# All element-wise sums on one engine, an unused set of sums left out, and a new order drawn by the kernel's own planner

## The chip, the core and the metric
The kernel runs on one core of a Trainium2 chip. The core has five engines with instruction streams of their own: TensorE (PE in the profile, with PEld for its weight loads), VectorE (DVE), ScalarE (ACT), GpSimd (POOL) and SyncE (SP). They meet through semaphores. SBUF is the working memory of 128 partitions, PSUM takes the results of TensorE in eight banks, and transfers from and to the chip's main memory run on 16 DMA engines. The metric is the device time of one execution in microseconds (us).

## The reference
Attention over 8 batches, 12 heads, 448 tokens and a head dimension of 64 is followed by two dense layers with a silu gate between them.
```python
scores = scale * np.matmul(q, k.transpose(0, 1, 3, 2))
attn = exp(scores - max) / (sum + 1e-09)
x = np.matmul(attn, v)            # -> (8 * 448, 768)
h = x @ w_in                      # w_in 768 x 2048
g = h * (1.0 / (1.0 + np.exp(-h)))
out = g @ w_out                   # w_out 2048 x 768
```
Inputs and output are float32; the kernel computes its products in float16 with float32 sums.

## The kernel before
**Tiling.** Attention works on *units*: one batch and four of the heads, 27 units in all, since batch 0 is cut into two pieces of tokens. For a unit, K and Q are loaded (rk, rq), turned on VectorE into KT and QT (L363, L374), multiplied on TensorE into scores (s, L384), and put through exp on ScalarE into tiles E (L409). Each unit has four chunks of keys and so four E tiles. TensorE then multiplies E with a matrix of ones for the row sums and with V for the result (p, L433); VectorE turns the row sums, inverts them, turns them back (t, inv; L455 to L460), and scales the result into xT (L466). Where there is room, the E tiles of chunks 0 and 1 are added first, so that the row sums need one chunk less: that is `plan_esum`, one sum for each half of the heads, 896 columns each.

**First layer.** `Plain` multiplies xT with w_in (p, L486) tile by tile; ScalarE takes tanh (th, L499) and VectorE the gate (G and X, L502).

**Second layer.** `Quad` makes a block of two times 128 tokens by 768 outputs with seven products for eight (a Strassen scheme). It needs sums of G tiles (S, or E tiles used for S, in `plan_sums`, four kinds of two sums of 512 columns each) and sums of w_out (TO and, in place, w_out_t, in `plan_w_out_sums`, 16 sums of 768 columns). Its results are added on VectorE (t<-p,t and p<-p,t, L511) or copied out of PSUM by ScalarE or VectorE (L515, L517), and stored by SyncE (L546). A similar scheme for the first layer, `Fold`, exists in the code with its sums of w_in (SI and, in place, w_in_t, in `plan_w_in_sums`, 32 sums of 384 columns), but it is for batches from `PLAIN` = 8 on, and there are eight batches, 0 to 7: no Fold runs.

**Order.** The program's instructions are put out in an order that a planner in the kernel draws at build time. `Order` keeps a clock for each engine; every `Op` has a cost, dependencies and a bias. TensorE is given work by the main loop: score products when they are ready and the pace allows, then attention results, then the first open item of the two layers. Each engine then runs its instructions strictly in the order put out, except for waits on semaphores. Kinds of operations in the planner: "DVE", "ACT", "POOL", "ANY" (ScalarE or VectorE) and "VP" (VectorE or GpSimd, whichever is free first in the planner). In the kernel before, E sums (`ESENG`), sums of weights (`WENG`) and the third and fourth kind of S sums (`VPS`) are "VP". All sums go through one helper, `tt`, so all have line L511; they are told apart by their tiles.

**Loads.** All loads are issued by GpSimd, in one list (`plan_k`, `plan_q`, `plan_v`, `plan_w_in`, `plan_w_out`), when nothing else is ready for GpSimd in the planner. The planner takes a load to land 1.5 us and size/0.37 after its issue or after the one before it, and 1.0 later; sizes of K and Q are multiplied by 1.2. w_out is loaded in two halves, in front of unit `W_OUT_AT` (12) and `W_OUT_AT + W_OUT_GAP` (14).

Of the kernel before, what the change touches and what calls it, by code (L numbers as in the profile page):

```python
# [17 lines left out]
HOP = 0.10  # L18
DMA_RATE = 0.37
DMA_TAIL = 1.0  # L20
# [3 lines left out]


# [54 lines left out]
class Op:  # L80


    def __init__(self, eng, busy, emit, deps=(), bias=0.0, tail=HOP, then=None, table=None):
        self.eng, self.busy, self.emit = eng, busy, emit
        self.deps, self.bias, self.tail, self.then = list(deps), bias, tail, then
        self.table = table
        self.done = None
# [5 lines left out]
class Order:  # L93


    def __init__(self):
        self.now = 0.0
        self.free = {"PE": 1.2, "ACT": 2.1, "DVE": 1.2, "POOL": 1.2}
        self.wait = {"ACT": [], "DVE": [], "ANY": [], "POOL": [], "VP": []}
        self.pool = []  # L100
        self.dma_free = 0.0
        self.out = []
        self.mode = None
        self.table, self.loose = 0, True
        self.busy = {e: 0.0 for e in self.free}

    def add(self, op):
        self.wait[op.eng].append(op)
        return op

# [3 lines left out]
    def start(self, op, eng=None):  # L114
        eng = eng or op.eng
        busy = op.busy[eng] if isinstance(op.busy, dict) else op.busy
        if isinstance(op.busy, dict):
            self.emit(lambda: op.emit(eng))
        else:
            self.emit(op.emit)  # L120
        if op.table is not None:
            if op.table != self.table:
                self.table = op.table
                busy += TABLE
        self.free[eng] = self.now + busy
        self.busy[eng] += busy
        op.done = self.now + busy + op.tail
        if op.then:
            op.then(op.done)
# [7 lines left out]
    def load(self, mb, emit, ring=None):  # L137
        op = Op("POOL", 0.58, emit)
        self.pool.append((op, mb, ring))
        return op  # L140

    def step(self):

        soon = []
        for eng in ("ACT", "DVE"):
            if self.free[eng] > self.now:
                soon.append(self.free[eng])
                continue
            best, other = None, None
            for kind in (eng, "ANY") if eng == "ACT" else (eng, "ANY", "VP"):  # L150
                for op in self.wait[kind]:
                    at = op.ready()
                    if at is None:
                        continue
                    if at > self.now:
                        soon.append(at)
                    elif eng == "ACT" and op.table not in (None, self.table):
                        if (other is None or at < other[0]) and (self.table == 0 or self.loose):
                            other = (at, op)
                    elif best is None or at + op.bias < best[0]:  # L160
                        best = (at + op.bias, op)
            if other:
                best = other if not best or self.table == 0 and other[0] < self.now - PATIENCE else best
                if best is not other:
                    soon.append(other[0] + PATIENCE + 0.01)
            if best:
                self.wait[best[1].eng].remove(best[1])
                self.start(best[1], eng)
                soon.append(self.free[eng])
        work = None  # L170
        for kind in ("POOL", "VP"):
# [12 lines left out]
        elif self.pool:  # L184
            op, mb, ring = self.pool[0]
            at = 0.0
            if ring is not None:
                at = ring()
            if at is not None and at <= self.now:
                self.pool.pop(0)  # L190
                self.start(op)
                self.dma_free = max(self.dma_free, self.now + 1.5) + mb / DMA_RATE
                op.done = self.dma_free + DMA_TAIL
                soon.append(self.free["POOL"])
            elif at is not None:
                soon.append(at)
# [4 lines left out]
def kernel(  # L201
# [10 lines left out]

# [20 lines left out]
    DEFER, DITEM = .3, .1  # L233
    SUMS, EKEEP, ESENG = (0, 1), 2, 'VP'
# [9 lines left out]
    W_OUT_AT = NG * len(PIECES) + 6  # L244
    W_OUT_GAP = 2
# [21 lines left out]
    SI = {m: const.tile([128, HC, DFF // 2], FP16, name=f"SI{m}") for m in (1, 2, 4)}  # L267
# [5 lines left out]
    T_s = const.tile([128, 3, HC, S // 2], FP16, name="T")  # L273
    f_s = [const.tile([128, 3, S // 2], FP32, name=f"f_{i}") for i in range(NF)]
# [7 lines left out]
    def bank(i):  # L282
        return P_s[i // 2][:, 0] if i < 4 else B_s[i - 4]
# [16 lines left out]
    def rows_of(n, c):  # L300
        return KROWS[c] if form(*units[n][:2]) == "lone" else 128

# [114 lines left out]
    def attend(n, part, a, es, sums):  # L417
# [6 lines left out]
        for c in chunks:  # L424
            rest = c == NCH - 1 and what != "lone"
# [159 lines left out]
    def plan_k(b, hg):  # L585
        ld_k[(b, hg)] = od.load(1.2 * MB * TPP, lambda: load_k(b, hg), ringed("rk"))

    def plan_q(n):
        ld_q[n] = od.load(1.2 * MB * (units[n][3] - units[n][2]), lambda: load_q(n), ringed("rq"))
# [101 lines left out]
    VPS = (3, 4)  # L691
    WENG = 'VP'
# [14 lines left out]
    def bulk(out, u, w, how, deps, bias):  # L707
# [7 lines left out]
        return od.add(Op(WENG, busy, lambda eng: tt(out, u, w, how, eng), deps, bias))  # L715
# [34 lines left out]
    plan_w_in_sums()  # L750
# [3 lines left out]
    class Quad:  # L754
# [59 lines left out]
        def run(self):  # L814
# [5 lines left out]
            if m == 5:  # L820
# [3 lines left out]
                "PE", (i1 - i0) * mm(n), lambda: self.emit(m, a, m in (1, 5, 6), i0, i1), tail=PE_OUT  # L824
# [13 lines left out]
            def add(name, out, x, y, deps, then=None):  # L838
                ev[name] = od.add(
                    Op("DVE", vec(n), lambda: tt(out, x, y, ALU.add), deps, SLOW, then=then)  # L840
                )

            if m == 1:
                ev["p1"] = od.add(
                    Op("ANY", {"ACT": act(n), "DVE": vec(n)}, lambda e: copy(e, p, W), [op], SLOW)
# [5 lines left out]
            elif m == 6:  # L851
                add("y", W, Q, r, [op, ev["c11"]])
            elif m == 7:
# [9 lines left out]
    class Fold:  # L863
# [66 lines left out]
        def run(self):  # L930
# [14 lines left out]
            op = Op("PE", HC * mm(n), lambda: self.emit(m, a, c0, m in (1, 7)), tail=PE_OUT)  # L945
# [3 lines left out]
            def add(name, eng, out, u, w, how, deps, then=None):  # L949
                busy = vec(n) if eng == "DVE" else 0.12 + 0.00215 * n  # L950
                ev[name] = od.add(
                    Op(eng, busy, lambda: tt(out, u, w, how, eng), deps, SLOW, then=then)
# [3 lines left out]
            if m == 5:  # L956
# [4 lines left out]
                        lambda e: copy(e, F[:, 0:2], src), [op], SLOW,  # L961
                    )
                )
            elif m == 6:
                add("y", "DVE", y, A[:, n : 2 * n], p1, ALU.add, [op])
# [3 lines left out]
            elif m == 3:  # L969
                c12 = add("c12", "DVE", A[:, n : 2 * n], A[:, n : 2 * n], p1, ALU.add, [op])  # L970
                self.finish(A[:, 0 : 2 * n], self.f, [c12], True)
            elif m == 4:
                Bq = bank(self.banks[1])[:, 0:n]
                k = self.banks[1]
                c21 = add("c21", "DVE", p5, Bq, p5, ALU.add, [op, ev["z"]], lambda at: banks.give(k, at))
                self.finish(F[:, 1:3].rearrange("p i n -> p (i n)"), self.f + HF, [c21], False)
            if m in (6, 7) and self.at >= 5 and "c22" not in ev:
                Bq = bank(self.banks[1])[:, 0:n]
                add("c22", "DVE", y, Bq, y, ALU.add, [self.last7, ev["y"]] + [ev["z"]])

        def finish(self, src, ff, deps, psum):
# [9 lines left out]
            if b < SILU:  # L991
# [4 lines left out]
                        -0.3, tail=0.2, table=0,  # L996
# [3 lines left out]
                for lo, hi, dst, at in g_parts(b, 0, S):  # L1000
# [7 lines left out]
                            [last, clear], -4,  # L1008
# [5 lines left out]
            for lo, hi, dst, at in g_parts(b, 0, S):  # L1014
# [6 lines left out]
                        deps + [clear], -2, tail=0.2, table=1,  # L1021
# [14 lines left out]
    def plan_t(b):  # L1036
# [12 lines left out]
        def sums(out, u, w, deps):  # L1049
            return od.add(  # L1050
                Op("DVE", half(HC * n), lambda: tt(out, u, w, ALU.subtract), deps, SLOW + 2)
# [40 lines left out]
    def plan_sums(qd):  # L1092
# [7 lines left out]
        while sums_at[qd] < 4:  # L1100
# [16 lines left out]
            for f0 in (0, 4):  # L1117
# [9 lines left out]
                else:  # L1127
# [7 lines left out]
                        deps, SUM,  # L1135
# [7 lines left out]
    def tile_quad(qd):  # L1143
# [34 lines left out]
        def write(r, c, src, place, deps, then):  # L1178
            if r == 0:
# [5 lines left out]
                        deps, -4,  # L1185
# [21 lines left out]
    class Plain:  # L1207
# [20 lines left out]
        def run(self):  # L1228
# [4 lines left out]
            op = Op("PE", 2 * mm(t1 - t0), lambda: ffn1_plain(b, f, t0, t1, a, c0, c0 + 2), tail=PE_OUT)  # L1233
# [7 lines left out]
            done = od.add(Op("ACT", act(t1 - t0), lambda: tanh(x, th), [op], -0.3, tail=0.2, table=0))  # L1241
# [5 lines left out]
            for lo, hi, dst, at in g_parts(b, t0, t1):  # L1247
# [5 lines left out]
                    [done], -4,  # L1253
# [38 lines left out]
    def qk_at():  # L1292
# [6 lines left out]
        s = [max(banks.free[2 * y], banks.free[2 * y + 1]) for y in ys]  # L1299
# [5 lines left out]
    def run_qk():  # L1305
# [17 lines left out]
        )  # L1323
        done = []
# [8 lines left out]
        for y in ys:  # L1333

            def then(at, y=y):
# [11 lines left out]
                    table=0,  # L1347
                )
# [3 lines left out]
        if c in SUMS and c == SUMS[-1] and per_burst(n) == 1 and ys[-1] == 1:  # L1352
            plan_esum(n)
# [3 lines left out]
    def plan_esum(n):  # L1357
# [3 lines left out]
        at = sum_at[n] = e_slots.take(od.now)  # L1361
        made = sum_op[n] = []
        kr = rows_of(n, SUMS[-1])
        nq = 32 * (units[n][3] - units[n][2])
        for y in range(2):
            hs = slice(2 * y, 2 * y + 2)
            for i, c in enumerate(SUMS[1:]):
                u = e_at[n][SUMS[0]] if i == 0 else at
# [5 lines left out]
                            lambda eng, u=u, w=e_at[n][c], hs=hs: tt(  # L1374
                                E_s[at][0:kr, hs, 0:nq], E_s[u][0:kr, hs, 0:nq],
                                E_s[w][0:kr, hs, 0:nq], ALU.add, eng,
                            ),
                            deps, -2,
# [6 lines left out]
    def lent():  # L1385
        if not qk_seq or silu_phase() or LEND and e_slots.when(1) is None:
            return 0, 2
# [9 lines left out]

    def m_when(n):
        more = lent()
        at = sorted(banks.free[i] for i in (*M, *more))[n - 1]  # L1400
        return None if at == NEVER else at

    def m_take():
        more = lent()
        i = min((*M, *more), key=lambda i: (banks.free[i] > od.now, i < 4, banks.free[i]))
        assert banks.free[i] <= od.now
# [3 lines left out]
    def av_data():  # L1410
# [7 lines left out]
        if part == 0 and n in sum_op:  # L1418
            first = len(SUMS) - 1
# [18 lines left out]
    def run_av():  # L1438
# [5 lines left out]
        sums = SUMS if n in sum_op else ()  # L1444
        count = NCH - (len(sums) - 1 if sums and part == 0 else 0)
        op = Op("PE", count * mm(nq) + 0.013, lambda: attend(n, part, a, es, sums), tail=PE_OUT)
# [18 lines left out]
    def after_av(n, part, op, nq, a):  # L1465
        b, hg, g0, g1 = units[n]
        if part == 0:
# [3 lines left out]
            for step, busy in enumerate((nq / 960.0 + 0.13, 0.2, nq / 960.0 + 0.13)):  # L1471
# [5 lines left out]
                    -10,  # L1477
                )
# [4 lines left out]
        else:  # L1483
# [5 lines left out]
            def then(at):  # L1489
# [10 lines left out]
                then=then,  # L1500
            )
# [35 lines left out]
    def moe_pick(hold):  # L1537
# [3 lines left out]
        for item in moe[:60]:  # L1541
# [10 lines left out]
            at = max([at] + room)  # L1552
            need = 0
# [12 lines left out]
        return None, soon  # L1566

# [70 lines left out]
    for _, _, fn in sorted(od.out, key=lambda x: x[:2]):  # L1638
# [31 lines left out]
```

## Time and profile before
| what | us |
|---|---|
| median of 3 runs | 447.63 (444.66 to 449.26) |
| the profiled execution | 442.18 |
| its span in the profile | 440.4 |
| TensorE busy | 410.0 |
| VectorE busy | 288.6 |
| ScalarE busy | 233.8 |
| GpSimd busy | 209.3, of which sums 109.2 and issues of loads the most of the rest |
| granted TensorE clock, mean | 0.979 of full |

The profile gives for each group of instructions its line, engine and operation, output and input tiles, and shape. "Idle before, releaser" is the time in which the engine stood in front of such an instruction, and whose end let it go. Instructions of one engine overlap a little, so durations can add up to more than the time from one start to the next. An instruction's duration includes what it stood inside the engine for a shared resource, which no wait in the list shows.

### The profile page before, as it was taken

The page shows a single profiled execution, that of the slowest core. Times are in us where ns is not written, and L with a number is a line of the kernel's source. Part 1 is how long each engine was busy: PE and PEld are TensorE (multiplying, and loading weights), DVE is VectorE, ACT ScalarE, POOL GpSimd, SP SyncE. Part 2 cuts the span into 40 slices and gives each one's busy share as a digit, 9 for nine tenths or more (in the row PEclk, how much of TensorE's full clock was granted, in tenths as well). Part 3 has the DMA queues.
Part 4 walks back from the last instruction along what each step waited for, and adds up shares of the span by engine and source line. Part 5 has one row for each costly group of instructions (what it writes and reads, how often), then busy time and mean ns, then how long its engine had stood idle before and what let it go on. Part 6 is the DMA issues. An engine that isn't in the chain of part 4 may idle for free.

```text
span 440.4 us, 9748 instructions
## 1 busy us (share of the span) xinstructions
PE 410.0 (93%) x3853; PEld 208.8 (47%) x3853; DVE 288.6 (66%) x565; ACT 233.8 (53%) x356; POOL 209.3 (48%) x277
## 2 busy tenths in 40 slices
PE   8998878999939999999999999999999999899985
PEld 7665544334315434544554434544453555455453
DVE  3536798777899776577557974587559635834751
ACT  3885757788800768466544755456856124214310
POOL 6575898977686354087204951065306100502510
PEclk9998989899988999999999999999999999999999
DMA  7999408599914456056510853118300130022023
GB/s 111 118 152 204 67 6 106 75 183 151 201 28 69 115 89 117 1 75 106 106 49 12 122 93 84 28 18 128 75 1 2 49 92 5 19 66 61 0 50 95
DMA packets 38750, 34.46 MB, mean 78 GB/s; under 512 B 11952, under 2 KB 37936, under 8 KB 38704
## 3 DMA queue, kind: packets, MB, share of 16 engines
q0 software_dynamic: 27952, 22.82, 37.0%
q1 hardware_dynamic: 9984, 10.24, 8.6%
q10 hardware_dynamic: 768, 0.79, 0.7%
q8 instruction: 30, 0.49, 0.4%
q14 instruction: 16, 0.13, 0.1%
HBM read 45.61 MB, written 11.01 MB: 129 GB/s over the span
## 4 chain that ended last, share of the span: by engine, by line
PE 60%; DVE 5%; DMA 2%; SPq 1%; issue 1%; POOL 1%; ACT 0%; DVEq 0%
PE p L486 24%; PE p L805 24%; PE p L433 7%; PE s L384 4%; DVE S L511 2%; DMA rk<-in_k_dram 1%; DVE E L511 1%; SPq L546 1%; DMA out_dram<-t 1%; DVE t L511 0%; POOL V L330 0%; DVE p L511 0%; DVE QT L374 0%; DVE G L502 0%; ACT th L499 0%
## 5 line engine op out<-in xcount | busy, mean ns | idle before, releaser
L409 ACT ACTIVATE E<-s 128x896 f16<-128x896 f32 (+1 forms) x172 | 148.6, 916 | 68.3 <-PE s L384 67.3
L486 PE MATMUL p<-xT,w_in_t 128*128 128x448 f16 (+1 forms) x864 | 156.9, 335 | 4.2 <-DVE G L502 3.2
L486 PEld LDWEIGHTS <-w_in_t 128*128 128x128 f16 x864 | 82.1, 99 | 76.9 <-issue 19.1
L502 DVE SCALAR_TENSOR_TENSOR G<-th,p 128x448 f16<-128x448 f16 (+2 forms) x144 | 75.7, 534 | 54.6 <-ACT th L499 54.1
L499 ACT ACTIVATE th<-p 128x448 f16<-128x448 f32 (+1 forms) x144 | 70.4, 507 | 63.7 <-PE p L486 60.5
L805 PE MATMUL p<-w_out_t,G 128*128 128x384 f16 x304 | 58.0, 327 | 1.9 <-DVE p L511 1.9
L384 PE MATMUL s<-QT,KT 32*128 32x448 f16 (+4 forms) x864 | 56.7, 343 | 3.0 <-ACT E L409 2.6
L511 POOL TENSOR_TENSOR G<-G 128x512 f16<-128x512 f16 x21 | 25.6, 1227 | 64.9 <-DVE S L511 64.3
L805 PEld LDWEIGHTS <-G 128*128 128x128 f16 x416 | 38.6, 98 | 36.1 <-issue 12.0
L330 POOL DMA_DIRECT2D V<-in_v_dram x88 | 48.9, 562 | 13.7 <-PE p L433 8.4
L515 ACT COPY t<-p 128x384 f32<-128x384 f32 x39 | 18.6, 479 | 69.3 <-PE p L805 67.0
L805 PE MATMUL p<-TO,S 128*128 128x384 f16 x192 | 39.3, 340 | 11.1 <-DVE S L511 7.6
L433 PE MATMUL p<-E,V 128*32 128x448 f16 (+2 forms) x848 | 43.9, 344 | 1.4 <-DVE xT L466 1.4
L805 PEld LDWEIGHTS <-S 128*128 128x128 f16 x280 | 25.8, 100 | 37.7 <-issue 15.5
L511 POOL TENSOR_TENSOR E<-E,E 128x896 f16<-128x896 f16 x18 | 34.6, 1922 | 18.0 <-ACT E L409 17.6
L511 DVE TENSOR_TENSOR t<-p,t 128x384 f32<-128x384 f32 x42 | 23.0, 549 | 29.3 <-PE p L805 26.6
L466 DVE SCALAR_TENSOR_TENSOR xT<-p,t 128x448 f16<-128x448 f32 (+1 forms) x53 | 29.8, 565 | 13.4 <-PE p L433 12.3
L384 PEld LDWEIGHTS <-KT 32*128 32x128 f16 (+2 forms) x864 | 17.6, 98 | 30.7 <-issue 29.0
L433 PEld LDWEIGHTS <-V 128*32 128x32 f16 (+1 forms) x864 | 20.3, 98 | 22.5 <-issue 12.4
L363 DVE STREAM_TRANSPOSE KT<-rk 128x256 f32<-128x256 f32 (+3 forms) x48 | 16.7, 385 | 19.6 <-DMA rk<-in_k_dram 19.6
L511 POOL TENSOR_TENSOR G<-X,G 128x512 f16<-128x512 f16 x4 | 4.9, 1216 | 46.2 <-DVE S L511 46.2
L455 DVE STREAM_TRANSPOSE t<-p 128x448 f32<-128x448 f32 (+1 forms) x27 | 15.9, 589 | 14.2 <-PE p L433 14.0
(62 smaller groups left out, 358.2 us busy)
## 6 DMA issues: line engine op xcount, KB each, us to landing
out_dram<-t SPq DMA_DIRECT2D x208, 48.0 KB, 1.6
rk<-in_k_dram POOLq DMA_DIRECT2D x24, 224.0 KB, 4.7
rq<-in_q_dram POOLq DMA_DIRECT2D x21, 224.0 KB, 5.4
w_out_t<-in_moe_w_out_dram POOLq DMA_DIRECT2D x8, 384.0 KB, 8.9
V<-in_v_dram POOLq DMA_DIRECT2D x43, 64.0 KB, 3.3
V<-in_v_dram POOLq DMA_DIRECT2D x40, 48.0 KB, 2.7
w_in_t<-in_moe_w_in_dram POOLq DMA_DIRECT2D x16, 96.0 KB, 4.7
w_in_t<-in_moe_w_in_dram POOLq DMA_DIRECT2D x8, 192.0 KB, 8.0
```

The lines of the kernel that those rows point to most:

```text
L330: nc.gpsimd.dma_start(out=V[32 * x : 32 * (x + 1), hs, 0:count, :], in_=v[b, hs].rearrange("h (i g) d -> i h g d", g=TPP)[:, :, first : fi ...
L363: nc.vector.transpose(out=kt.rearrange("p c x i -> p x c i")[:, x:y, 0:count], in_=t[:, first : first + count * (y - x)].rearrange("p (x c ...
L384: nc.tensor.matmul(out=P_s[s_pair][p0 : p0 + 32 * (x1 - x0), h % 2, at : at + nq], lhsT=KT[(b, hg)][32 * h : 32 * (h + 1), c, x0:x1, :, e] ...
L409: nc.scalar.activation(out=E_s[e_i][0:kr, 2 * y : 2 * y + 2, 0:nk], in_=P_s[s_pair][0:kr, :, 0:nk], func=AF.Exp, scale=attn_scale,)
L433: nc.tensor.matmul(out=bank(a)[32 * h : 32 * (h + 1), 0:nq], lhsT=w, rhs=E_s[sum_at[n] if part == 0 and c in sums else es[c // per_burst(n)]][
L466: nc.vector.scalar_tensor_tensor(out=x_s[xi][:, cc % HC, 32 * g0 : 32 * g1], in0=bank(a)[:, 0:nq], scalar=0.5, in1=t_s[ti][:, 0:nq], op0=A ...
L486: nc.tensor.matmul(out=bank(a)[:, 0 : t1 - t0], lhsT=w_in_t[:, cc, 128 * f : 128 * (f + 1)], rhs=x_s[x_at[(b, cc // HC)]][:, cc % HC, t0:t ...
L499: nc.scalar.activation(out=th, in_=src, func=AF.Tanh)
L502: (nc.vector if eng == "DVE" else nc.gpsimd).scalar_tensor_tensor(out=out, in0=th, scalar=1.0, in1=x, op0=ALU.add, op1=ALU.mult)
L511: e.tensor_tensor(out=out, in0=a, in1=b, op=op)
L515: nc.scalar.copy(out=out, in_=in_)
L805: nc.tensor.matmul(out=bank(a)[:, 0 : self.n], lhsT=lhs(i), rhs=rhs(i), start=(start and i == 0), stop=(i == last), skip_group_check=True,)
```

## The change
1. `ESENG` and `WENG` go from 'VP' to 'DVE', and `VPS` is empty: all sums are on VectorE.
2. `plan_w_in_sums` is called only if `PLAIN < B`, which is false; SI, T and f tiles aren't made.
3. The planner takes a load to land 2.4 us and size/0.4 after its issue, without the later 1.0 and the factor of 1.2, and has at most 8 loads open (`DMA_OPEN`).
[...]
5. w_out is loaded in front of unit 11 and unit 12.
6. E sums are planned by `sums_of` (chunks 0 and 1 for units from 6 on); `DEFER` goes from 0.3 to 0.15; four banks of the score tiles are lent at the end instead of two.

```diff
-DMA_RATE = 0.37
-DMA_TAIL = 1.0
+DMA_RATE = 0.4
+DMA_LAG = 2.4
+DMA_OPEN = 8
...
+    def locked(self, tiles, eng):
+
+        return max((t for i in tiles for e, t in self.lock[i].items() if e != eng), default=0.0)
...
+                    elif self.locked(op.tiles, eng) > self.now:
+                        soon.append(self.locked(op.tiles, eng))
+                    elif eng == "DVE" and op.port and self.port["POOL"] > self.now:
+                        soon.append(self.port["POOL"])
...
-            if ring is not None:
+            if len(self.sent) >= DMA_OPEN and self.sent[-DMA_OPEN] > self.now:
+                at = self.sent[-DMA_OPEN]
+            elif ring is not None:
                 at = ring()
...
-                self.dma_free = max(self.dma_free, self.now + 1.5) + mb / DMA_RATE
-                op.done = self.dma_free + DMA_TAIL
+                self.dma_free = max(self.dma_free, self.now + DMA_LAG) + mb / DMA_RATE
+                op.done = self.dma_free
+                self.sent.append(op.done)
...
-    DEFER, DITEM = .3, .1
-    SUMS, EKEEP, ESENG = (0, 1), 2, 'VP'
+    DEFER, DITEM = .15, .1
+    EKEEP, ESENG = 2, 'DVE'
+    ES2 = 99
+    ES0, ES1 = 6, 99
...
-    W_OUT_AT = NG * len(PIECES) + 6
-    W_OUT_GAP = 2
+    W_OUT_AT = NG * len(PIECES) + 5
+    W_OUT_GAP = 1
...
+    def sums_of(n):
+        if per_burst(n) == 2 or n < ES0:
+            return ()
+        return (0, 1) if n < ES1 else (0, 1, 2) if n < ES2 else (0, 1, 2, 3)
...
-        ld_k[(b, hg)] = od.load(1.2 * MB * TPP, lambda: load_k(b, hg), ringed("rk"))
+        ld_k[(b, hg)] = od.load(MB * TPP, lambda: load_k(b, hg), ringed("rk"))
...
-    VPS = (3, 4)
-    WENG = 'VP'
+    VPS = ()
+    WENG = 'DVE'
...
-    plan_w_in_sums()
+    if PLAIN < B:
+        plan_w_in_sums()
     plan_w_out_sums()
...
         if not qk_seq or silu_phase() or LEND and e_slots.when(1) is None:
-            return 0, 2
+            return 0, 1, 2, 3
```

## The prediction
> **What bounds the kernel now.** I read the table of busy times first, then the busy time of every engine in stretches of 20 us, then the waits, and at each stretch in which TensorE stands, the timeline of the engine it waits for.
>
> ```profile
> PE 410.0 (93%) x3853; PEld 208.8 (47%) x3853; DVE 288.6 (66%) x565; ACT 233.8 (53%) x356; POOL 209.3 (48%) x277
> ...
> PEclk9998989899988999999999999999999999999999
> ```
> TensorE is the bound: 410 of 440.4 us. No other engine is above two thirds. So a faster kernel can only come from the 30.4 us in which TensorE stands, or from the clock, which the second row shows below full speed in single slices of the first third only.
>
> ```profile
> 0.00:20.00 20.00, 17.67 (x317) 14.53 (x321) 7.38 (x26) 11.91 (x14) 10.70 (x23) 1.00 0.83 113
> ...
> 60.00:80.00 20.00, 15.90 (x176) 7.81 (x175) 16.97 (x36) 12.11 (x20) 18.25 (x25) 0.84 0.55 72
> 80.00:100.00 20.00, 20.00 (x222) 7.60 (x214) 14.48 (x33) 15.96 (x23) 16.51 (x25) 0.99 0.97 140
> ...
> 120.00:140.00 20.00, 13.03 (x88) 6.85 (x77) 19.32 (x25) 2.45 (x5) 15.49 (x14) 0.83 0.28 43
> ...
> 420.00:440.40 20.40, 14.12 (x85) 8.10 (x83) 6.93 (x13) 2.39 (x5) 0.93 (x1) 0.96 0.32 78
> ```
> Columns: stretch, length, then busy us of PE, PEld, DVE, ACT, POOL, then granted clock, DMA share, GB/s. TensorE lacks 4.1 us in 60 to 80 and 7.0 us in 120 to 140, both times with VectorE (17.0, 19.3) and GpSimd (18.3, 15.5) nearly full, and both times the clock falls to 0.83 or 0.84. The first 20 us (2.3 lacking, loads at 0.83 of the DMA engines) and the tail (6.3, the last sums and stores) are a matter of start and end.
>
> ```profile
> 121.78 8.40 DVE L511 TENSOR_TENSOR w_out_t<-w_out_t 128x768 f16<-128x768 f16 x1
> 130.11 0.55 DVE L511 TENSOR_TENSOR TO<-w_out_t,TO 128x768 f16<-128x768 f16 x1
> ```
> ```profile
> 121.53 1.64 POOL L511 TENSOR_TENSOR TO<-w_out_t,TO 128x768 f16<-128x768 f16 x1
> 123.13 1.87 POOL L511 TENSOR_TENSOR E<-E,E 128x896 f16<-128x896 f16 x1
> 124.96 1.62 POOL L511 TENSOR_TENSOR TO<-w_out_t,TO 128x768 f16<-128x768 f16 x1
> 126.55 1.62 POOL L511 TENSOR_TENSOR w_out_t<-w_out_t 128x768 f16<-128x768 f16 x1
> 128.14 1.62 POOL L511 TENSOR_TENSOR TO<-w_out_t,TO 128x768 f16<-128x768 f16 x1
> ```
> ```profile
> 131.04 0.82 PE L805 MATMUL p<-TO,S 128*128 128x384 f16 x2 [6.97 <-DVE S L511]
> ```
> This is the heart of it. Start, duration, instruction. A sum over 768 columns takes VectorE 0.55 us; the one that began at 121.78 took 8.40 us and ended 0.4 us after the last of a row of GpSimd sums (128.14 + 1.62 = 129.76). The two S sums queued behind it, and TensorE stood 6.97 us for the first. A VectorE sum of two SBUF tiles waits for GpSimd's sums to stop.
>
> **The change, part by part.** Counts are from the two programs' orders, durations from the groups with shapes apart.
>
> *Sums leave GpSimd.* 82 sums, 109.2 us (groups E 34.6, G 25.6 + 4.9, S 9.3 + 2.4, w_in and SI 18.6, w_out and TO 10.1, E of FFN2 3.7). 20 of them and 12 on VectorE (8.3 us) make SI and the difference in w_in, which no matmul reads: they go. The other 62 go to VectorE: 20 of E at 0.61 us (the sum at 71.06, before GpSimd began one) = 12.2; 38 of 512 columns at 0.41 = 15.6; 6 of 768 at 0.55 = 3.3. Ten copies out of PSUM also go from ScalarE to VectorE, 10 x 0.545 = 5.5. Together +36.6.
>
> *VectorE's own sums get short.* Mean now less the unhindered duration, times the count: E 18 x (1.213 - 0.61) = 10.9; S<-S,G 20 x (0.835 - 0.41) = 8.5; S<-G 24 x 0.145 = 3.5; w_out 10.5 - 3 x 0.55 = 8.9; the smaller groups 5.8. Sum 37.6. So VectorE's total goes 288.6 + 36.6 - 8.3 - 37.6 = 279, and GpSimd's to about 100: VectorE takes over all sums and is busy for less.
>
> *What of it is TensorE's.* Stalls with a GpSimd sum as their cause, from the timelines of the three engines:
> - 124.1 to 131.0: 6.97, shown above.
> - 59.5 to 62.7: 3.20. The gates (G, L502) stood behind two SI sums of 3.01 us together, held up by POOL's own SI and E sums. These SI sums are unused.
> - 48.3 to 50.0: 1.66, for an E sum on GpSimd (1.87 us; on VectorE 0.61).
> - 380 to 384.5 and 416 to 422: 1.94, 0.58 and 1.59. Behind the last gate of a batch, VectorE does eleven sums before the addition that TensorE waits for; three of each set took 1.37 us against GpSimd's. New order: ten sums at 0.34 from start to start, 3.4 us instead of 5.5. TensorE has 5.2 us of other products there, so I count all 4.1.
> - 251 to 256: 1.06 (an E sum pair of 2.22 us).
> Sum 17.0. To this the clock: after the stall at 131.04, 16 products took 4.69 us where twice 8 take 2.6 (-2.0); after 62.66, 1.3 us more than the same products elsewhere. -3.3. TensorE's own work stays: 3853 to 3832 matmuls, of which 17 are idle filler at the start; switches between the row, column and full forms are 253 and 250 in the two orders.
>
> [...] The row says that VectorE stayed out over five GpSimd sums in a row. [...]
>
> [...] All loads here are issued by GpSimd, and VectorE will do 62 more sums. [...]
>
> *Order with the loads.* GpSimd's stream of loads is the same list, but for w_out, whose first half goes one unit of attention earlier and whose second half two. The cap of 8 and the new rates work only in the planner. It now believes in a k load (0.459 MB in float32) after 2.4 + 0.459/0.4 = 3.5 us, before 4.0; the trace has a median of 4.7 (rq 5.4). So the turns of K and Q stand as early or earlier in VectorE's queue, with gates, S and xT behind them. Now VectorE waits 19.6 us for rk and 2.8 for rq, 16 times. Bounds: it falls to half, since POOL's sums no longer stand in front of the loads (in 50 to 60 the DMA share was 0.01 with POOL 10.0 of 10 busy): -1 on TensorE; or it grows by 27 x 0.5 = 13 us, of which I let TensorE feel a third: +4. I take +1.5. One unit more gets its E sum: 4 matmuls less, -0.2. DEFER, the bank locks and the two more lent banks change which product comes next: -1 to +3, I take +1.5, about the 1% of stalls that the undisturbed stretch from 140 to 376 has (3 us).
>
> Sum: 442.2 (the profiled execution: span 440.4 and 1.8 around it) - 17.0 - 3.3 + 3.0 = 424.9. The three runs shown lie above their profiled one (median 447.6, by 1.2%). Part of that is these blockades, which fall differently in every run; I add nothing but round: **425 us**, 5% under the median.
>
> **Rivals.**
> 1. *The early stage is bound by its loads.* From 84 to 118 the DMA share is above 0.9 in nearly every slice; all of w_out is fetched there beside K, Q and V. If so, TensorE freed at 48 to 63 runs into K and Q that aren't there and gives the 4.9 us and 1.3 us of clock back, and w_out makes the seven at 124 half as large: 425 + 6.2 + 3.5 = 435. For it: w_out now comes with one unit between its halves, 16 us of transfers. Against: in 50 to 60 nothing was being fetched, and TensorE waited 0.3 us in all for a load.
> 2. *Slower.* VectorE, in order, stands at each K and Q turn for a load that the planner believed in 1.2 (k) to 1.9 us too early, and now has every sum behind it. Place: the first turn of each of the 21 whole units. Price: if each costs TensorE 1.6 us, 34 us against 20 gained: 456 in the profiled sum's terms, 460 as a median. It decides from about 1.0 us a unit on, where the gain is eaten. Against: VectorE has 160 us of slack, and with today's 22 us of such waits no wait of TensorE behind a KT or QT row is above 0.4 us.
> 3. *Nothing moves.* TensorE's work is the same, and VectorE's stalls are replaced by ScalarE's: from 40 to 120 ScalarE is busy 60.5 of 80 us, and squeezed into 68 it would be 89%. Then 440 to 446. Against: the new order puts second-layer products, which need no exponentials, into this stage.
>
> **How the numbers follow.** Forecast 0.62 (418 to 432), loads 0.20 (428 to 442), nothing moves 0.09 (440 to 450), slower 0.09 (450 to 465). The range reaches from 415 (the -1 bounds, and the slow clock of 74 to 80 gone too, 3 us, with some 4 us of small waits on VectorE) to 440, the loads' case nearly whole. 1% of the median, 4.5 us, is about what a measurement of this kernel tells from no change: faster (below 443.2) 0.84, within 0.08, slower (above 452.1) 0.08.
>
> **What would show it.** Right: no VectorE sum above 0.7 us; VectorE near 280 and GpSimd near 100 us busy; no stall of TensorE above 2 us between 30 and 425; clock 1.00 in all 20 us stretches after 40. Loads: VectorE's wait for rk above 30 us in the first 130 us. Rival 2: waits of TensorE behind KT or QT rows in every batch. Wrong altogether: a stall as long as those removed with GpSimd idle.

## The result and the profile after

The changed kernel takes 421.08 us (median of 3 runs, 416.86 to 423.8) against 447.63: a ratio of 0.9369, 95% interval 0.9208 to 0.953. A ratio given with an interval is taken from the executions counted as fast alone, so it need not equal the quotient of the medians beside it. Measured again with more runs, the changed kernel takes 421.48 against 445.02, 0.9505 (0.9451 to 0.956). The two intervals share 0.945 to 0.953; I take the gain as about 5%. The profiled execution of the changed kernel (416.86, span 415.1) is the fastest of its three, with a mean granted clock of 0.996, and that of the kernel before (442.18) lies below its three runs.

The table of busy times after, then the rows by stretches of 20 us that answer to those shown before (stretch, length, busy PE, PEld, DVE, ACT, POOL, granted clock, DMA share, GB/s):

```profile
PE 402.2 (97%) x3832; PEld 207.2 (50%) x3832; DVE 274.6 (66%) x627; ACT 229.6 (55%) x346; POOL 101.0 (24%) x195
...
PEclk9899999999999999999999999999999999999999
```
```profile
0.00:20.00 20.00, 16.48 (x246) 13.60 (x246) 6.47 (x24) 8.75 (x10) 9.51 (x21) 0.91 0.79 106
...
60.00:80.00 20.00, 19.96 (x241) 9.40 (x242) 16.25 (x41) 17.20 (x27) 9.68 (x17) 1.00 0.73 103
80.00:100.00 20.00, 19.44 (x184) 8.23 (x176) 17.24 (x41) 13.43 (x20) 9.30 (x17) 1.00 1.15 181
...
120.00:140.00 20.00, 20.00 (x226) 8.27 (x226) 16.42 (x38) 14.37 (x18) 7.59 (x15) 1.00 0.74 117
```
TensorE stands 415.1 - 402.2 = 12.9 us instead of 30.4, of which 3.5 lie in the first 20 us and 4.8 behind 400 us. From 60 to 80 it works 19.96 us of 20 where it worked 15.9. VectorE does all sums and is busy for 14 us less than before.

The sums of one line and engine in the changed kernel: count, then shortest/median/longest in ns, first and last start.

```profile
L541 DVE TENSOR_TENSOR E<-E,E x38: 584/616/626, 39.4 to 319.1; 128x896 f16<-128x896 f16 x38
L541 DVE TENSOR_TENSOR S<-S,G x20: 382/418/426, 70.9 to 395.8; 128x512 f16<-128x512 f16 x20
...
L541 DVE TENSOR_TENSOR w_out_t<-w_out_t x4: 551/556/559, 95.7 to 101.5; 128x768 f16<-128x768 f16 x4
```
The longest equals the median within a few per cent in each group. Before, the w_out sum ranged to 8398 ns. What is left of TensorE's waits from 40 us on, in order of size (us in total, times, longest):

```profile
PE p L516 <- DMA rk<-in_k_dram: 1.1, 1, 1.1
PE p L516 <- DVE G L532: 0.9, 1, 0.9
PE p L516 <- DVE X L532: 0.8, 2, 0.5
PE p L836 <- DVE p L541: 0.8, 1, 0.8
```
None is above 1.1 us, and none has a GpSimd sum behind it.

### The profile page after: what moved, and what is told of

The parts are those of the page before. It is cut to its first block, busy times and chain, and to the rows that moved or that the text cites. A ratio compares the mean times of both kernels' runs of the same rounds, so it can differ in the third digit from the quotient of the medians.

```text
span 415.1 us, 9668 instructions
## 1 busy us (share of the span) xinstructions
PE 402.2 (97%) x3832; PEld 207.2 (50%) x3832; DVE 274.6 (66%) x627; ACT 229.6 (55%) x346; POOL 101.0 (24%) x195
## 4 chain that ended last, share of the span: by engine, by line
PE 84%; DMA 8%; DVE 3%; POOL 2%; issue 1%; ACT 1%; ACTq 0%; DVEq 0%; POOLq 0%
PE p L516 33%; PE p L836 29%; PE p L463 12%; PE s L414 10%; DMA rk<-in_k_dram 4%; DMA V<-in_v_dram 2%; DMA rq<-in_q_dram 2%; POOL V L360 1%; DVE KT L393 1%; DVE G L532 1%; DVE t L541 0%; DVE xT L496 0%; DMA out_dram<-t 0%; PE s L463 0%; ACTq L576 0%
## 5 line engine op out<-in xcount | busy, mean ns | idle before, releaser
L516 PEld LDWEIGHTS <-w_in_t 128*128 128x128 f16 x864 | 81.1, 98 | 74.5 <-issue 14.9
L836 PE MATMUL p<-w_out_t,G 128*128 128x384 f16 x304 | 59.0, 327 | 0.8 <-DVE p L541 0.8
L463 PE MATMUL p<-E,V 128*32 128x448 f16 (+2 forms) x832 | 42.1, 337 | 2.3 <-DMA V<-in_v_dram 1.6
L545 ACT COPY t<-p 128x384 f32<-128x384 f32 x29 | 13.9, 480 | 44.2 <-PE p L836 42.0
L836 PE MATMUL p<-TO,S 128*128 128x384 f16 x192 | 36.6, 327 | 0.2 <-DVE t L541 0.2
L463 PEld LDWEIGHTS <-V 128*32 128x32 f16 (+1 forms) x864 | 20.5, 98 | 22.4 <-issue 10.3
L359 POOL MEMSET V<- 64x256 f16 x20 | 6.1, 305 | 81.9 <-PE p L463 81.5
L541 DVE TENSOR_TENSOR E<-E,E 128x896 f16<-128x896 f16 x38 | 22.9, 615 | 0.2 <-ACT E L439 0.2
L836 PE MATMUL p<-TO,G 128*128 128x384 f16 x112 | 21.5, 326 | 0.0
```

Source lines behind the costliest of these rows:

```text
L463: nc.tensor.matmul(out=bank(a)[32 * h : 32 * (h + 1), 0:nq], lhsT=w, rhs=E_s[sum_at[n] if part == 0 and c in sums else es[c // per_burst(n)]][
L516: nc.tensor.matmul(out=bank(a)[:, 0 : t1 - t0], lhsT=w_in_t[:, cc, 128 * f : 128 * (f + 1)], rhs=x_s[x_at[(b, cc // HC)]][:, cc % HC, t0:t ...
L541: e.tensor_tensor(out=out, in0=a, in1=b, op=op)
L836: nc.tensor.matmul(out=bank(a)[:, 0 : self.n], lhsT=lhs(i), rhs=rhs(i), start=(start and i == 0), stop=(i == last), skip_group_check=True,)
```

## The experiments

**One part of the change at a time.** The theory: a VectorE sum of two SBUF tiles is held up by GpSimd's sums, and that is the cause of TensorE's stalls. Rivals: the unused sums are in the way, or the redrawn order does it.

All sums on VectorE, the unused ones too, in the kernel before:

```diff
-    SUMS, EKEEP, ESENG = (0, 1), 2, 'VP'
+    SUMS, EKEEP, ESENG = (0, 1), 2, 'DVE'
-    VPS = (3, 4)
-    WENG = 'VP'
+    VPS = ()
+    WENG = 'DVE'
```


> The kernel before with one part of the change: all sums on VectorE (the 32 unused w_in sums too), order drawn with the old load times. Blocking by GpSimd as the cause: no VectorE sum above 0.7 us, the 7.0 us stall before the second layer gone, ratio 0.95 to 0.97 of before. If the unused sums are the cause: they now burden VectorE by 32 x 0.35 = 11 us, ratio 0.99 to 1.01. If load times and order are the cause: 0.98 to 1.01.

Measured: 425.29 against 445.08, ratio 0.9572 (0.9506 to 0.9638). This is inside the first theory's range; moving the sums alone makes most of the change. In its trace, no unused sum takes above 358 ns, and from 60 to 82 us the longest VectorE sum of two SBUF tiles takes 0.62 us.

Only the unused sums dropped (`plan_w_in_sums` behind `if PLAIN < B`), the rest on either engine as before:

> The kernel before without the 32 unused sums of w_in; the other sums stay on either engine. Blocking as the cause: the stalls at 48 and 59 us go (4.9 us and 1.3 of clock), VectorE sums of several us remain elsewhere, ratio 0.98 to 0.99. Unused sums as the cause: 0.95 or less. Order as the cause: 0.99 to 1.00.

Measured: 445.67 against 445.08, ratio 1.0005 (0.9968 to 1.0042). The blocking theory's range, 0.98 to 0.99, doesn't hold it; the order's, 0.99 to 1.00, does, and the next two runs decide on the order. Of the two stalls that I had expected to go, that at 59 us, behind SI sums, is gone; that at 48 us, for an E sum on GpSimd, is still there and longer, 2.9 us behind a sum from 47.50 to 49.37. Other stalls have come in their place. One of them, in the timelines of VectorE, GpSimd and TensorE (start, duration, instruction):

```profile
114.83 3.67 DVE L511 TENSOR_TENSOR TO<-w_out_t 128x768 f16<-128x768 f16 x1
118.42 0.63 DVE L460 STREAM_TRANSPOSE t<-inv 128x448 f32<-128x448 f32 x1
118.98 0.44 DVE L502 SCALAR_TENSOR_TENSOR G<-th,p 128x320 f16<-128x320 f16 x1
```
```profile
112.67 3.58 POOL L511 TENSOR_TENSOR TO<-w_out_t 128x768 f16<-128x768 f16 x2
116.21 1.86 POOL L511 TENSOR_TENSOR E<-E,E 128x896 f16<-128x896 f16 x1
```
```profile
119.67 2.72 PE L806 MATMUL p<-TO,S 128*128 128x384 f16 x8 [3.13 <-DVE X L502]
```
A TO sum of VectorE now stands until the second of GpSimd's two sums and its E sum are over (116.21 + 1.86 = 118.07), and the inverse and the gates behind it make TensorE late by 3.13 us. TensorE stands 443.0 - 410.7 = 32.3 us in that execution, 30.4 before. Which VectorE sum meets a GpSimd sum is drawn anew with each order; that some do is what costs.

Only the planner's load times, its limit of 8 open loads and the place of w_out:

```diff
-DMA_RATE = 0.37
-DMA_TAIL = 1.0
+DMA_RATE = 0.4
+DMA_LAG = 2.4
+DMA_OPEN = 8
...
-    W_OUT_AT = NG * len(PIECES) + 6
-    W_OUT_GAP = 2
+    W_OUT_AT = NG * len(PIECES) + 5
+    W_OUT_GAP = 1
```


> The kernel before with only the planner's load times, the limit of 8 open loads and w_out one and two units earlier. Blocking as the cause: GpSimd sums as many and as long, ratio 0.99 to 1.01. Order as the cause: 0.95 to 0.97.

Measured: 446.35 against 445.08, ratio 1.008 (1.0034 to 1.0126). The medians are 1.3 us apart, within the spread of either kernel, so this is no change or a slight loss; TensorE has two stalls behind gates of 4.8 and 4.4 us. An order redrawn by the load times gains nothing while GpSimd's sums stand.

Sums moved and unused ones dropped, old planner and load times:

> All sums on VectorE and the unused ones left out, with the old load times and old planner. Blocking as the cause: nearly all of the whole change's gain, ratio 0.94 to 0.955. Order as the cause: at least 3% is missing, 0.97 or more.

Measured: 420.65 against 445.08, ratio 0.946 (0.9393 to 0.9527). That is about the changed kernel's time, without its planner. Beside the first of these runs, on the same chip, dropping the unused sums is worth 425.29 - 420.65 = 4.6 us, although alone it was worth nothing. On VectorE the 32 sums are 11 us of work; with them, VectorE is busy for 18.62 of the 20 us from 60 to 80 and TensorE works 17.79, without them 16.76 and 18.73. So, in the orders that were drawn, the two parts work together: the unused sums cost when they stand on VectorE.

**The rest of the change, taken back from the other end.** The changed kernel with the old load times, no limit and w_out at its old place:

> The changed kernel with the old load times in the planner, no limit of open loads and w_out at its old place. If load times matter little: within 1% of the changed kernel, ratio 0.935 to 0.95 of before. If they carry the gain: 0.965 or more, with stalls of TensorE behind late loads.

Measured: 422.65 against 446.52, ratio 0.9477 (0.9432 to 0.9521). The load times carry none of the gain that can be seen. The changed kernel and the old planner with the two edits were then measured side by side on one chip:

> The changed kernel as it is, on the chip of the three runs beside it. Ratio 0.935 to 0.95 of before. If the new load times and planner rules are worth anything beyond the sums: at least 0.5% below the run with only the sums moved and the unused ones dropped.

> The kernel before with all sums on VectorE and the unused ones dropped, old planner, again, beside the changed kernel. If the order is worth nothing: within 0.5% of the changed kernel, either way. If the order carries a part: 0.5 to 1.5% above it.

Measured: 421.48 and 421.63, ratios 0.9505 and 0.9507. The redrawn order, the planner's rules `locked` and `port`, which put waits for other engines into the plan, the load times, and the bank and w_out changes show no gain: the medians are 0.15 us apart, where the six executions of each kernel spread over 4 to 5 us. A small worth of the order isn't excluded, because the granted clocks differ: 0.959 to 0.983 in the changed kernel's executions, 0.982 to 0.995 in the other's. The one execution of the changed kernel with a clock of 0.996 is that of the first profile, with 416.86, and the other kernel's with 0.995 took 419.56.

The changed kernel with its sums of E, w_out and part of S back on either engine, and with the planner's rule `port`, which keeps VectorE's and GpSimd's sums from overlapping in the plan:

```diff
-    EKEEP, ESENG = 2, 'DVE'
+    EKEEP, ESENG = 2, 'VP'
-    VPS = ()
-    WENG = 'DVE'
+    VPS = (3, 4)
+    WENG = 'VP'
```


> The changed kernel with the sums of E, w_out and the third and fourth S back on whichever engine is free, the planner's port model on. If a planner that keeps the two apart avoids the blocking: ratio 0.94 to 0.955 and no VectorE sum above 2 us. If real times drift from planned ones so that sums meet all the same: VectorE sums of 1.5 us and more come back, 0.96 to 0.98.

Measured: 428.35 against 446.52, ratio 0.9571 (0.9492 to 0.9651). It is 5.7 us slower than the changed kernel with the old load times (422.65), measured on the same chip with all sums on VectorE. By ratio it lies between the two expectations; by its sums the second was right. Shortest/median/longest in ns:

```profile
L541 DVE TENSOR_TENSOR S<-S,G x20: 361/416/2430, 72.5 to 408.9; 128x512 f16<-128x512 f16 x20
L541 DVE TENSOR_TENSOR E<-E,E x13: 577/615/1804, 46.0 to 331.6; 128x896 f16<-128x896 f16 x13
```
Medians are near those of the changed kernel (418 and 616), the longest are not: the planner keeps most sums apart, and some still meet. That real times drift from planned ones would explain it, but it was not looked at. With all sums on one engine nothing has to be kept apart: 426 and 626 ns are the longest of these groups in the changed kernel.

**The blockade by itself.** The changed kernel, and on GpSimd six sums in a row that nobody reads, started by VectorE's first TO sum. The order of every other engine is that of the changed kernel.

```diff
+    def row(t1):
+        for i in range(6):
+            nc.gpsimd.tensor_tensor(out=ROW[i], in0=t1, in1=t1, op=ALU.add)
```


> The changed kernel plus six sums of 768 columns in a row on GpSimd that start when VectorE's first TO sum is done and that nobody reads; the order of all other engines is unchanged. If VectorE stays out until GpSimd's row ends: one VectorE sum takes 8 to 10 us. [...]

The timelines of VectorE, GpSimd and TensorE there:

```profile
99.94 0.55 DVE L542 TENSOR_TENSOR TO<-w_out_t 128x768 f16<-128x768 f16 x1
100.72 0.49 DVE L533 SCALAR_TENSOR_TENSOR G<-th,p 128x320 f16<-128x320 f16 x1 [0.23 <-ACT th L530]
101.12 0.28 DVE L533 SCALAR_TENSOR_TENSOR X<-th,p 128x128 f16<-128x128 f16 x1
101.32 8.51 DVE L542 TENSOR_TENSOR TO<-w_out_t 128x768 f16<-128x768 f16 x1
109.76 0.47 DVE L533 SCALAR_TENSOR_TENSOR G<-th,p 128x320 f16<-128x320 f16 x1
```
```profile
100.84 8.57 POOL L770 TENSOR_TENSOR ROW<-TO 128x768 f16<-128x768 f16 x6
```
```profile
109.89 0.80 PE L844 MATMUL p<-TO,S 128*128 128x384 f16 x2 [7.27 <-DVE TO L542]
```
The two gates at 100.72 and 101.12 run beside GpSimd's row in 0.49 and 0.28 us, where the changed kernel's take 482 and 277 ns on average; of their two inputs, p is in PSUM. The sum of two SBUF tiles stands from 101.32 to 109.83, 0.42 us past the end of all six GpSimd sums (100.84 + 8.57 = 109.41). It got in between none of them, and the trace shows no wait for data in front of it. The stall of the kernel before is made again: 7.27 us of TensorE.

The control has the same place, a sum of 2 columns and then 16 memsets:

```diff
+    def row(t1):
+        nc.gpsimd.tensor_tensor(out=ROW[0][:, 0, 0:2], in0=t1[:, 0, 0:2], in1=t1[:, 0, 0:2], op=ALU.add)
+        for i in range(16):
+            nc.gpsimd.memset(ROW[i % 6], 0.0)
```


> The same place, but one sum of 2 columns and then 16 memsets of 768 columns on GpSimd, which read no tile, for about as long. If it is reads by GpSimd that hold VectorE off: no VectorE sum above 0.7 us behind the first. If any GpSimd work holds it off: one of several us as with the row of sums.

Its timelines of VectorE and GpSimd:

```profile
100.88 0.55 DVE L542 TENSOR_TENSOR TO<-w_out_t 128x768 f16<-128x768 f16 x1
101.35 0.48 DVE L533 SCALAR_TENSOR_TENSOR G<-th,p 128x320 f16<-128x320 f16 x1
101.75 0.28 DVE L533 SCALAR_TENSOR_TENSOR X<-th,p 128x128 f16<-128x128 f16 x1
101.94 0.55 DVE L542 TENSOR_TENSOR TO<-w_out_t,TO 128x768 f16<-128x768 f16 x1
```
```profile
100.43 10.93 POOL L771 MEMSET ROW<- 128x768 f16 x16
```
GpSimd is busy for longer, 10.9 us, and no sum is hindered: 0.55 us each. So GpSimd being busy with memsets, which write SBUF, did not keep VectorE out; its sums, which also read SBUF, did, for 8.51 us. A GpSimd operation with one input was not run. The single times are 432.72 with the row of sums and 424.8 with the memsets, at granted clocks of 0.956 and 0.958: 7.9 us apart, about the length of the stall.

**Looking for more.** The dropped tiles leave room in SBUF, and GpSimd stood 8.5 us in front of one K load for a free buffer. Four raw buffers for K and Q instead of two, and beside it also 12 E tiles and 8 t tiles:

```diff
-        t = sb.tile([128, TPP, D], FP16, name=f"rk_{b}_{hg}", tag="rk", bufs=2)
+        t = sb.tile([128, TPP, D], FP16, name=f"rk_{b}_{hg}", tag="rk", bufs=4)
...
-    NE, NX, NTMP, NSG, NF, NTH, NK = 9, 4, 6, 3, 1, 4, 2
+    NE, NX, NTMP, NSG, NF, NTH, NK = 12, 4, 8, 3, 1, 4, 2
```


> The changed kernel with four buffers each for raw K and raw Q instead of two, in the room that the dropped tiles leave. If what is left early is a matter of loads that wait for a free buffer (GpSimd stood 8.5 us before one K load and 7.2 before Q loads): VectorE's wait for rk and rq falls below 15 us from 30, 2 to 4 us less than the changed kernel. If the loads themselves are the limit there: same within 0.5%.

> As before it, with 12 E tiles instead of 9 and 8 t tiles instead of 6. If room for E holds the order back: 1 to 3 us below the run with more raw buffers alone. If TensorE is the bound from 45 us on: no difference above 0.5%.

Measured: medians 424.64 and 425.27, beside 421.48 for the changed kernel. These medians can't be compared as they stand, because each falls on executions with a low granted clock. At clocks of 0.990 to 1.0, the two kernels took 415.81, 416.83 and 417.19, and the changed kernel 416.86 at 0.996; at clocks near 0.96, they took 424.9 to 426.2, and the changed kernel 422.9 to 423.8. No gain shows. GpSimd's waits for a free raw buffer all but go, but VectorE's wait for K and Q falls only to 19.4 + 2.2 us, not below 15; an execution of the changed kernel at the same low clock has 21.0 + 3.9.

## Why the prediction was right, point by point

Forecast 425, measured 421, and 5 to 6% under the median where 5% was forecast. The cause is the one forecast: VectorE's sums, held up by GpSimd's, made TensorE stand. The sizes are partly luck. In the terms of the working, from profiled execution to profiled execution, 424.9 was forecast and 416.86 measured, 8.0 us less: TensorE's standing time was forecast to fall by 17.0 - 3.0 = 14.0 us and fell by 17.5, and its busy time by 3.3 and fell by 7.8. The medians come nearer because the execution that was profiled has a higher clock, 0.996, than any of the other eight on record for the changed kernel (0.959 to 0.983). That the blockades fall differently in every run was my guess: it is not shown, as the timelines of before are of one execution.

- *Where the sums go and what they cost.* Forecast 279 us of VectorE and about 100 of GpSimd; measured 274.6 and 101.0. No sum above 0.7 us: the longest of two SBUF tiles is 626 ns.
- *TensorE's stalls, 17.0 us.* The standing time fell by 30.4 - 12.9 = 17.5, although the loads added about 3 (below). So some 3 us more went than I had listed, in small waits: those behind ScalarE's exponentials, for one, fell from 2.6 us to 0.4. The attribution of single stalls was too fine. Before its own run I booked 4.9 us at 48 to 63 to the unused SI sums as if those were an item of their own; with them alone gone, TensorE stood 32.3 us. The listed stalls all went since all GpSimd sums went together. GpSimd being the slower engine (an E sum takes it 1.92 us on average, and VectorE 0.62 in the changed kernel) is a smaller part: of TensorE's waits before, one of 1.7 us was directly for a GpSimd sum.
- *The end of the last two batches.* Nine and ten sums instead of eleven, in part slow, ones: 3.8 us from the first of them to the addition, at 360.53 and 396.89, where I had 3.4. TensorE has its products without a gap, and the 4.1 us are gained.
- *The clock, -3.3.* This is the term that was mis-sized. I counted it only in the first products behind two stalls. TensorE's busy time fell by 7.8 us; the rows by stretch (length times what the clock lacks of 1.00, an estimate) give 1.8 + 3.2 + 3.4 + 0.8 = 9.2 us lost to the clock before (20 to 40, 60 to 80, 120 to 140, the end), and 1.8 in the changed kernel's profiled execution. Clock 1.00 in all stretches after 40 us held in that execution; in its second profile 40 to 60 has 0.86, and it holds from 60 on.
- *The loads, +1.5.* VectorE's waits for K and Q went up from 22.4 us to 30.3, inside my bounds, and TensorE felt 1.7 us between 40 and 45, plus 1.6 for a V load at 15, where it had waited 0.3 us for loads before. That is twice the 1.5 that I took, but inside the bounds of -1 and +4; in the second profile TensorE waits for no load at all.
- *The order, +1.5.* No loss shows: the run with the old planner is 0.15 us away, at a higher clock.
- *The row at 121.78 as a rule.* I read it as the rule that a VectorE sum waits for GpSimd's sums to stop. As a rule that was wrong. In the trace of before, 11 VectorE sums that had to wait had a further GpSimd sum close behind: in 10 cases VectorE got in after the first one, and GpSimd's next sum was delayed instead. The row at 121.78 is the eleventh. One of the ten, from the timelines of GpSimd and VectorE, with GpSimd's two sums and VectorE's between them:

```profile
131.87 1.40 POOL L511 TENSOR_TENSOR G<-G 128x512 f16<-128x512 f16 x1 [2.10 <-DVE S L511]
132.18 1.50 DVE L511 TENSOR_TENSOR w_out_t<-w_out_t 128x768 f16<-128x768 f16 x1
133.23 1.95 POOL L511 TENSOR_TENSOR TO<-w_out_t,TO 128x768 f16<-128x768 f16 x1
```
VectorE's sum ends at 133.68, 0.41 us after the first GpSimd sum (133.27), and the second takes 1.95 us instead of 1.62. With only the unused sums dropped, VectorE got in behind such a first sum three times between 96 and 128 us (the sums that began at 113.03, 119.55 and 120.54), and the one that began at 114.83 stood over two. What decides between the two was not found. The forecast didn't suffer, because it counted stalls that the trace had; of the 17.0 us, only the 7.0 depend on the long row.
- *GpSimd's issues of loads*, beside 62 more sums on VectorE: V issues take 558 ns on average with all sums on VectorE, 562 before, and rk issues 565 and 572. No slowing shows.
- *The rivals.* Early loads are not the gain either, as VectorE waited longer for K and Q than before. The loads' case would have shown as VectorE waiting over 30 us for K in the first 130 us: 25.0 in the whole span. The slower case needed TensorE standing behind KT or QT: none of its waits from 40 us on is put down to one. ScalarE's case: TensorE waits 0.4 us for it.

## What to carry to other kernels

The sums that GpSimd took off VectorE weren't free here: 109 us of GpSimd sums made VectorE's own sums 37 us longer (the estimate of the prediction), which is more than doing the useful ones on VectorE (31 us). The blockade appeared in no list of VectorE's waits: the sum of 8.40 us has none in front of it. Look for a group whose longest instruction is many times its shortest (here 8398 ns against 553), and lay the other engine's timeline beside it. And test the parts of a change one at a time and together: the dead work was worth nothing while the blockade stood, and 4.6 us when it was gone.

## What the runs showed of the hardware that was not expected

In the trace of before, a VectorE sum of two SBUF tiles that met a row of GpSimd sums waited for one of them in 10 cases of 11. In the eleventh a sum of 768 columns, which takes 0.55 us alone, stood 8.40 us over a row of five, and one stood 8.51 us over the row of six that was added to the changed kernel.

The clock in the first 50 us differs between executions of one program. In the second profile of the changed kernel (span 421.1), the rows in stretches of 10 us are:

```profile
10.00:20.00 10.00, 10.00 (x146) 7.00 (x149) 4.19 (x12) 6.18 (x9) 3.38 (x7) 0.57 0.91 118
20.00:30.00 10.00, 10.00 (x138) 5.53 (x128) 3.42 (x9) 6.25 (x8) 8.51 (x16) 0.50 1.01 145
30.00:40.00 10.00, 10.00 (x120) 5.39 (x114) 4.08 (x12) 5.19 (x8) 5.41 (x11) 0.50 1.10 192
```
The granted clock, the seventh number behind the stretch, is 0.50 from 20 to 40 us with TensorE never idle, where the first profile has 1.00 in both rows. Up to 140 us TensorE is busy for 137.2 us, 132.9 in the first profile, and stands 2.8 us instead of 7.1: the 3.3 us of waits for loads that the first profile has are not in the second. The spans are 6.0 us apart (421.1 and 415.1). What sets the clock there was not tried: the starts of the two executions have the same products and the same filler. It bounds what can be told of this kernel by single runs to about 1.5%.
